# Seven block products in the first layer's second product, and second-layer weights used where they are made

## The chip, the cores and the metric

The kernel runs on one core of a Trainium2 chip. The metric is the device time of one execution in microseconds. A core has five engines with queues of their own, and each works through its queue in program order: TensorE (PE) multiplies matrices, VectorE (DVE), ScalarE (ACT) and GpSimd (POOL) work elementwise, SyncE (SP) issues the transfers between HBM and the on-chip memory SBUF. A matmul writes into one of eight PSUM banks of 128 x 512 fp32, from which ACT and DVE read.

## The reference

```python
def _moe_ref(x, w_in, w_out):                       # first layer, d_ff 2048
    h = x @ w_in
    g = np.maximum(h, 0.0) + np.log1p(np.exp(-np.abs(h)))     # softplus
    return (g @ w_out).astype(np.float32)

def _moe2_ref(x, w_gate, w_val, w_out):             # second layer, d_ff 1536
    g = x @ w_gate
    silu = g * (1.0 / (1.0 + np.exp(-g)))
    val = x @ w_val
    return (silu * val @ w_out).astype(np.float32)

def reference(**kwargs):                            # x (4,8,512,64), state (4,8,32,64)
    attn_out = _attn_ref(**attn_kwargs)             # attention of x and state, both ways
    B, H, S, D = attn_out.shape                     # 4, 8, 544, 64
    x = np.ascontiguousarray(attn_out.transpose(0, 2, 1, 3)).reshape(B * S, H * D)
    x = _moe_ref(x=x, **moe_kwargs)
    return _moe2_ref(x=x, **moe2_kwargs)
```

There are 2176 tokens: 4 batches of 512 positions, and 4 x 32 state rows. The weights come as 64-bit floats.

## The kernel before, in words

Every fp32 operand is split into a high and a low part of a type that PE takes at full rate, and a product is made of three matmuls, high by high, low by high and high by low (`mm3`, L87). All of PE's large products go through its line 90. The high part is a copy on ACT, the low part a subtraction on POOL or DVE (`low`, L92).

After the attention, the first layer runs over 4 chunks c of 512 hidden columns, 4 batches b and 4 tiles ft of a chunk: 64 units of 128 hidden columns by 512 positions. For each unit PE makes `p2` (12 matmuls: the softplus of one unit times a 128-row piece of w_out, into the four banks py, which stay open over the four units of a batch) and `p1` of the unit four steps ahead (6 matmuls into a bank ph). ACT takes the softplus of ph twice, as `h` (high part) and `C` (whole), and POOL subtracts to get `l`. At the end of each batch DVE adds the four banks py to the sums yacc in SBUF (`y_add`, L511). Each chunk also has, for every batch, an M pair (`m_pair`, L442: two groups pm of 8 small matmuls, of the chunk's w_in with the attention's state). Its two banks are one of the tag "m" and one of the tag "h", the tag from which ph takes its banks; ACT copies the high parts and DVE subtracts the low parts (`m_low`, L93) before the banks come free. Products for the state rows (ps) stand at fixed steps too.

Weights are converted in pieces of 128 x 512 by the class `Piece`: ACT scales the upper words (`size`, L135), DVE shifts and joins the words (`head`, L144; `tail`, L155 and L158), ACT and POOL split (L164, L93). 16 pieces each of w_in and w_out belong to the first layer. The second layer's 36 pieces (24 of gate and value, `GatePiece`, 12 of its w_out, `OutPiece`) are made during the first layer (18 of them) or in the first pass of the second (18, by a shorter form: ACT L133, DVE L139 and L151); gate pieces also get four sums of their quarters (L205). A made piece is written to HBM and loaded back when a step needs it (`load_gw`, `load_w2`).

The second layer has 24 steps n: 2 batch pairs by 12 tiles f. Each step makes its gate and value products as seven products of half-size blocks instead of eight (`quad_mm`, P1 to P7), in banks px, py and pz that DVE and ACT empty between them; its output products, too, go by seven parts in the second pass.

The order of work on each engine is the program's: a schedule written by hand. In the first layer `at(n, kind, ...)` hangs work on a unit, and the loop over units emits, for one unit, `p2`, the hooks "pe", `p1`, then for the other engines the softplus of the unit before, `y_add`, and the hooks "dve0", "act", "pool", "dve1" and so on. `M_STEPS` says at which unit of a chunk the M pairs stand. In the second layer `at2` does the same.

```python
    BUFS = {"y": 4, "h": 3, "m": 1}
    LAG = 4
    M_STEPS = (10, 12, 15, 19)
```

## Time and profile before

| | us |
|---|---|
| median of 3 runs | 732.83 (731.96 to 732.92) |
| the profiled execution | 732.92 |
| its span in the profile | 731.1 |
| PE busy | 710.4 (97%) |
| DVE busy | 484.2 (66%) |
| POOL busy | 412.6 (56%) |
| ACT busy | 331.0 (45%) |

The span is what the profiler records between the first and last instruction; 1.8 us of the execution lie around it. The attention takes the first 45 us or so, the first layer goes on to about 320 us, the second layer fills the rest. In the timeline a row that ends with x6 or x12 stands for so many instructions of one kind in sequence. The records of neighbouring instructions of one engine overlap a little, so the distance from start to start is the better measure of what an instruction costs.

### The profile page before, as it was taken

How to read it: one execution, taken by the hardware profiler on the slowest of the kernel's cores; microseconds unless marked ns; L12 is line 12 of the kernel's file. 1: busy time of each engine (PE TensorE's matmuls, PEld its weight loads, DVE VectorE, ACT ScalarE, POOL GpSimd, SP SyncE). 2: the span in 40 equal slices, each digit the busy share in tenths (PEclk: the TensorE clock that was granted, in tenths of full speed). 3: DMA queues.
4: the chain of work that ended last, by engine and by line, in shares of the span. 5: the costliest groups of instructions: out<-in, count | busy, mean ns of one | idle time of the engine just before them, and what ended most of it. 6: DMA issues, size and time to landing. Idle time of an engine off the chain costs nothing.

```text
span 731.1 us, 10299 instructions
## 1 busy us (share of the span) xinstructions
PE 710.4 (97%) x3690; PEld 569.6 (78%) x3690; DVE 484.2 (66%) x689; ACT 331.0 (45%) x612; POOL 412.6 (56%) x349
## 2 busy tenths in 40 slices
...
GB/s 342 408 129 10 48 115 138 201 205 179 162 131 189 188 120 161 161 301 0 122 280 330 373 362 278 327 260 337 207 251 386 345 338 279 296 144 328 168 12 116
DMA packets 55395, 159.54 MB, mean 218 GB/s; under 512 B 6192, under 2 KB 18480, under 8 KB 55344
## 3 DMA queue, kind: packets, MB, share of 16 engines
...
q14 instruction: 22, 0.18, 0.1%
...
## 4 chain that ended last, share of the span: by engine, by line
PE 85%; DVE 8%; POOL 2%; issue 2%; ACT 2%; DMA 1%; SPq 0%; ACTq 0%; DVEq 0%; POOLq 0%
PE py L90 24%; PE px L90 18%; PE po L90 10%; PE ph L90 10%; PE pz L90 9%; PE poP L90 7%; PE pt L90 3%; PE pm L432 2%; PE ps L90 1%; PE ps L565 1%; DMA st<-in_st_dram 1%; DVE t_wo L155 1%; DVE t L351 1%; DVE m L93 1%; DVE m L354 1%
## 5 line engine op out<-in xcount | busy, mean ns | idle before, releaser
L90 PE MATMUL py<-h,wo 128*128 128x512 f32 x512 | 159.1, 391 | 0.6 <-POOL wo L93 0.6
L93 POOL TENSOR_TENSOR l<-C,h 128x512 fp32r<-128x512 f32 x64 | 91.7, 1439 | 78.7 <-ACT C L465 61.9
L90 PEld LDWEIGHTS py<-h,wo 128*128 128x128 f32 x512 | 95.9, 188 | 22.2 <-POOL wo L93 1.4
L90 PE MATMUL ph<-aT,m 128*128 128x512 f32 x384 | 99.9, 396 | 2.7 <-DVE m L93 2.7
L90 PE MATMUL py<-l,wo 128*128 128x512 f32 x256 | 99.9, 390 | 0.0
L90 PEld LDWEIGHTS ph<-aT,m 128*128 128x128 f32 x384 | 70.5, 188 | 28.0 <-issue 5.9
L462 ACT ACTIVATE h<-ph 128x512 fp32r<-128x512 f32 x64 | 38.2, 598 | 108.4 <-PE py L90 101.6
L90 PE MATMUL po<-h,w 128*128 128x512 f32 x224 | 69.7, 392 | 0.0
L90 PE MATMUL px<-T_0s,gw 128*128 128x512 f32 x216 | 60.8, 390 | 0.5 <-ACT cA L1025 0.5
L90 PE MATMUL px<-T_1s,gw 128*128 128x512 f32 x216 | 60.7, 390 | 0.0
L90 PEld LDWEIGHTS py<-l,wo 128*128 128x128 f32 x256 | 48.1, 188 | 10.2
L643 DVE TENSOR_TENSOR oacc<-po,oacc 128x512 f32<-128x512 f32 x48 | 32.4, 687 | 27.9 <-PE po L90 27.8
L90 PEld LDWEIGHTS po<-h,w 128*128 128x128 f32 x224 | 41.6, 188 | 8.4
L93 POOL TENSOR_TENSOR gv<-t_gv,gv 128x512 fp32r<-128x512 f32 x24 | 32.4, 1348 | 27.4 <-ACT gv L164 27.2
L643 DVE TENSOR_TENSOR oacc<-poP,oacc 128x512 f32<-128x512 f32 x62 | 40.7, 686 | 10.3 <-PE poP L90 10.3
L90 PEld LDWEIGHTS px<-T_0s,gw 128*128 128x128 f32 x216 | 40.4, 188 | 9.1 <-ACT cA L1025 1.0
L90 PEld LDWEIGHTS px<-T_1s,gw 128*128 128x128 f32 x216 | 40.6, 188 | 8.4
L90 PE MATMUL po<-l,w 128*128 128x512 f32 x112 | 43.7, 390 | 0.0
L93 POOL TENSOR_TENSOR split_gv<-sums_gv,split_gv 128x512 fp32r<-128x512 f32 x24 | 33.1, 1378 | 17.2 <-ACT split_gv L209 16.5
L93 POOL TENSOR_TENSOR l<-cA,h 128x512 fp32r<-128x512 f32 x14 | 19.7, 1407 | 40.0 <-ACT h L629 39.8
L985 POOL TENSOR_TENSOR cC<-cC,cB 128x512 f32<-128x512 f32 x24 | 31.8, 1326 | 18.4 <-ACT cB L984 18.4
L1051 DVE TENSOR_TENSOR cA<-py,cA 128x512 f32<-128x512 f32 x22 | 15.2, 689 | 40.2 <-PE py L90 34.1
...
## 6 DMA issues: line engine op xcount, KB each, us to landing
...
```

The source lines that it names most:

```text
L90: nc.tensor.matmul(o, a[s], b[t], start=first and i == 0, stop=last and i == 2, **k)
L93: eng.tensor_tensor(out=o, in0=whole, in1=high.bitcast(F32), op=ALU.subtract)
L155: nc.vector.scalar_tensor_tensor(out=ti, in0=self.top, scalar=-0x80000000, in1=ti, op0=ALU.bitwise_and, op1=ALU.bitwise_or,)
L351: nc.vector.transpose(self.t, self.sc)
L354: nc.vector.tensor_reduce(out=self.mine("m1", 16), in_=self.t3, op=ALU.max, axis=AX.X)
L432: nc.tensor.matmul(ps[k * NS:(k + 1) * NS, :], st[q, k, b, :], win[c, k].t[q, :], start=True, stop=True)
L462: nc.scalar.activation(self.h, self.ps, AF.Softplus)
L565: nc.tensor.matmul(gs[c][:, f], win[c, kt].t[:, f], sw[:, kt, :], start=kt == 0, stop=kt == KT - 1)
L643: nc.vector.tensor_tensor(out=v, in0=ps, in1=v, op=ALU.add)
L985: nc.gpsimd.tensor_tensor(out=c["C"], in0=c["C"], in1=c["B"], op=ALU.mult)
L1051: nc.vector.tensor_tensor(out=c["A"], in0=y, in1=c["A"], op=ALU.add)
```

## The change

Three stretches of the first layer, each a chunk c and a pair q of batches, (1, 1), (2, 1) and (3, 0), no longer run `p2`. Of their eight units, seven make one block product each (`y_part`, 12 matmuls into two banks pyP), in the order P1, P2, P5, P3, P6, P7, P4, and the eighth makes none. The blocks are the hidden tiles 0, 1 against 2, 3 and the two batches of the pair. This takes sums of the softplus blocks, T1 to T4 (`g_sum`, on DVE, 24 in all), sums of w_out blocks (`WoSums`, on DVE), and their high and low parts on ACT and POOL. Where a batch's two second-batch units with ft < 2 are only used in sums, their own `h` and `l` are left out. Parts P1, P2 and P5 open banks, the others go on adding in a bank which another part has filled, after DVE has added its content to yacc (`y_part_add`).

Of the second layer's 36 pieces, 7 are made in the first layer instead of 18, and 29 in the second layer's first pass instead of 18; these stay in SBUF and are used from there in that pass, and written to HBM for the second pass. The M pairs move to other units and to two banks of the tag "m"; `p1` runs up to seven units ahead of the rest; weight loads start one unit later.

```diff
-    SLOTS = {"aT": 8, "mt": 8,  "wo": 6, "yacc": 8, "s": 2, "xT": 8, "T": 14, "made": 3, "w2": 4, "w2s": 4, "gw": 8}
+    SLOTS = {"aT": 10, "mt": 8,  "wo": 6, "yacc": 8, "s": 2, "xT": 8, "T": 14, "made": 3, "w2": 5, "w2s": 4, "ws": 6}
...
-    BUFS = {"y": 4, "h": 3, "m": 1}
+    BUFS = {"y": 5, "h": 5, "m": 2}
...
+            return "aT" if self.slope else "made"
+
         def low(self):
             super().low()
+            if self.slope:
+                gw[self.f, self.i, 0] = self.out
...
-                gw[n, i, kind] = slot([P, 2, 512], F32R, "gw", f"gw{n}_{i}_{kind}")
+                gw[n, i, kind] = slot([P, 2, 512], F32R, "aT", f"gw{n}_{i}_{kind}")
...
+        if (c, b // 2) in SEVEN and b % 2 and ft < 2:
+            sp[u] = Softplus(ps, g, None)
+        else:
+            sp[u] = Softplus(ps, g, work.tile([P, 512], F32R, tag="GH", bufs=BIG, name=f"h{n}"))
...
+    def y_put(b, dt, ps, first):
         if (b, dt // 2) not in yacc:
             yacc[b, dt // 2] = slot([P, 2, 512], F32, "yacc", f"yacc{b}_{dt // 2}")
         v = yacc[b, dt // 2][:, dt % 2, :]
-        if c == 0 and dt % 2:
-            nc.scalar.activation(v, yps[dt], AF.Copy)
-        elif c == 0:
-            nc.vector.tensor_copy(v, yps[dt])
+        if first and dt % 2:
+            nc.scalar.activation(v, ps, AF.Copy)
+        elif first:
+            nc.vector.tensor_copy(v, ps)
         else:
-            nc.vector.tensor_tensor(out=v, in0=yps[dt], in1=v, op=ALU.add)
+            nc.vector.tensor_tensor(out=v, in0=ps, in1=v, op=ALU.add)
...
+    SEVEN = {(1, 1), (2, 1), (3, 0)}
+    BIG = 16
+
+
+    OUTS = {
+        "P1": ("f0", 0, "B11"), "P2": ("f1", 0, "B21"), "P3": ("s", 3, "B22"), "P4": ("f1", 1, "T4"),
+        "P5": ("s", 0, "T1"), "P6": ("s", 1, "T2"), "P7": ("s", 2, "T3"),
+    }
+    KEEP = {"P1": "x", "P6": "x", "P7": "x", "P4": "x", "P2": "z", "P5": "z", "P3": "z"}
+    OPENS = ("P1", "P2", "P5")
+    TO = {"P1": (0, 0), "P2": (0, 0), "P5": (1, 1), "P6": (1, 0), "P3": (1, 0), "P7": (1, 1), "P4": (0, 1)}
...
+        x, y, op, at = {
+            "T1": ("B12", "B11", ALU.subtract, None), "T3": ("B22", "B12", ALU.subtract, "B12"),
+            "T2": ("T3", "B11", ALU.add, "B11"), "T4": ("B21", "T2", ALU.subtract, "B21"),
+        }[t]
+        a, b = (g_whole(c, q, k, f) for k in (x, y))
+        if at is None:
+            o = work.tile([P, 512], F32, tag="G", bufs=BIG, name=f"{t}_{c}_{q}_{f}g")
+        else:
+            o = g_whole(c, q, at, f)
+        nc.vector.tensor_tensor(out=o, in0=a, in1=b, op=op)
+        gsum[c, q, t, f] = o
...
+        nc.scalar.activation(h, gsum[c, q, t, f], AF.Copy)
+        gT[c, q, t, f] = (h, l)
+
+    def g_split_low(c, q, t, f, eng):
+        h, l = gT[c, q, t, f]
+        low(eng, l, gsum[c, q, t, f], h)
...
+    def y_part(c, q, part):
+        kind, k, t = OUTS[part]
+        keep = KEEP[part]
+        for i in range(2):
+            if part in OPENS:
+                ypx[keep, i] = bank("y", f"pyP{part}_{c}_{q}_{i}")
+            ps = ypx[keep, i]
+            cols = slice(k % 2 * 256 + i * P, k % 2 * 256 + (i + 1) * P)
+            for f in range(2):
+                if t in BLOCK:
+                    j, ft = BLOCK[t]
+                    g = gT[c, 2 * q + j, ft + f]
+                else:
+                    g = gT[c, q, t, f]
+                w = ws[c, k // 2, f] if kind == "s" else wo[c, 2 * int(kind[1]) + f].out
+                mm3(
+                    ps, [w[:, l, cols] for l in range(2)], g, part in OPENS and f == 0, f == 1,
+                    skip_group_check=True,
+                )
+
+    def y_part_add(c, q, part, i):
+        j, m = TO[part]
+        y_put(2 * q + j, 2 * m + i, ypx[KEEP[part], i], c == 0 and part in ("P1", "P5", "P6", "P4"))
...
+    SEQUENCE = ("P1", "P2", "P5", "P3", "P6", "P7", "P4", None)
     LAG = 4
-    M_STEPS = (10, 12, 15, 19)
-    with tc.manual_schedule(engines={ENG.PE}):
+    LEAD = [min(LAG + max(0, n - 11) // 2, 7) for n in range(64)]
+    M_STEPS = (7, 9, 12, 16)
...
-            at(max(0, n - 4), "load", begin)
+            at(max(0, n - 3), "load", begin)
...
+                if i in (5, 7) and SEVEN & {(c + 1, 0), (c + 1, 1)}:
+                    sums = WoSums(c + 1, i // 2 - 2)
+                    m = n + 2 if (c + 1, 0) in SEVEN else n + 7
+                    at(m, "dve1", sums.sums)
+                    at(m + 1, "act", sums.high)
+                    at(m + 1, "pool", sums.low)
             if c + 1 < NCK:
-                for b, i in enumerate(M_STEPS):
+                for b, i in enumerate(M_STEPS if c else (10, 11, 13, 17)):
...
-        EARLY = [(c * UC + n, 0) for c in range(NCK - 1) for n in ((2, 3, 6, 7, 10, 14) if c else (11, 14, 15))]
-        EARLY += [((NCK - 1) * UC + n, 0 if n % 4 else 2) for n in (0, 1, 2)]
-        for j, (n, late) in enumerate(EARLY):
-            at_weights(n, late, made, (j,), second_piece)
-            at(n + late + 1, "pool", lambda j=j: made[j,].sums())
-            at(n + late + 2, "act", lambda j=j: made[j,].split_sums())
...
+        for c, q in sorted(SEVEN):
+            m = c * UC + q * 2 * FT
+            for t, f, n, kind in (
+                ("T1", 0, -1, "dve2"), ("T1", 1, 0, "dve0"), ("T3", 0, 0, "dve2"), ("T2", 0, 1, "dve0"),
+                ("T3", 1, 1, "dve2"), ("T2", 1, 2, "dve0"), ("T4", 0, 2, "dve2"), ("T4", 1, 3, "dve0"),
+            ):
+                at(m + n, kind, g_sum, c, q, t, f)
+            for t, f, n in (
+                ("T1", 0, -1), ("T1", 1, 0), ("T2", 0, 1), ("T2", 1, 2), ("T3", 0, 2), ("T3", 1, 3),
+                ("T4", 0, 3), ("T4", 1, 4),
+            ):
+                at(m + n, "act1", g_split_high, c, q, t, f)
+                at(m + n, "pool1", g_split_low, c, q, t, f, nc.gpsimd)
+        EARLY = [(c * UC + n, 0) for c, n in ((1, 2), (1, 3), (1, 6), (2, 2), (2, 3), (2, 6), (3, 2))]
+        for key, (n, late) in zip(((0, 0), (0, 1), (1, 0), (1, 1), (2, 0), (2, 1), (0, 2)), EARLY):
+            at_weights(n, late, made, key, second_piece)
+            at(n + late + 1, "pool", lambda key=key: made[key].sums())
+            at(n + late + 2, "act", lambda key=key: made[key].split_sums())
...
+            done = FIRST + LAG - 1
+            fresh = []
             for n in range(FIRST, NU):
                 run(n, "load")
-                if True:
-                    u = units[n]
+                u = units[n]
+                c, q, k = u[0], u[1] // 2, n % (2 * FT)
+                seven = (c, q) in SEVEN
+                part = SEQUENCE[k] if seven else None
+                if part:
+                    y_part(c, q, part)
+                elif not seven:
                     p2(u)
-                    if n == FIRST:
-                        p1(units[n + LAG - 1])
-                    run(n, "pe")
-                    if n + LAG < NU:
-                        p1(units[n + LAG])
-                nx = units[n + LAG - 1] if n + LAG - 1 < NU else None
-                if nx:
-                    sp[nx].high()
-                    sp[nx].whole()
-                last = u[2] == FT - 1
-                for dt in range(KT) if last else ():
+                ready, fresh = fresh, []
+                if n == FIRST:
+                    p1(units[done])
+                    ready, done = [units[done]], done + 1
+                run(n, "pe")
+                while done < min(NU, n + LEAD[n] + 1):
+                    p1(units[done])
+                    fresh.append(units[done])
+                    done += 1
+                for v in ready:
+                    sp[v].high()
+                    sp[v].whole()
+                for dt in range(KT) if not seven and u[2] == FT - 1 else ():
                     y_add(u[0], u[1], dt)
                 run(n, "dve0")
+                if part:
+                    y_part_add(c, q, part, 0)
                 run(n, "act")
-                if nx:
-                    g_low(nx)
+                for v in ready:
+                    g_low(v)
                 run(n, "pool")
+                run(n, "dve2")
+                if part:
+                    y_part_add(c, q, part, 1)
...
+        for f in range(NF):
+            for part, t0 in enumerate((4 * f - 8, 4 * f - 7, 4 * f - 5 if f > 1 else 2)):
+                if (f, part) in made:
+                    continue
+
+                def begin(f=f, part=part):
+                    made[f, part] = second_piece(f, part, True)
+
+                at2(t0 // 4 - 1, "load", begin)
...
-        for q, n in enumerate((10, 12, 13, 14, 16)):
+        for q, n in enumerate((11, 12, 14, 16, 18)):
...
-                if n + 2 < NS2:
+                if n == 0 or NF <= n + 2 < NS2:
                     load_gw(n + 2)
-                if n % 2 and n + 1 < NS2:
+                if n % 2 and NF <= n + 1 < NS2:
...
```

PE, third unit of batch 2 of chunk 1 before the change (py1_2_3 is a bank of chunk 1, batch 2; pm2 the M pair of chunk 2; ph the first product):

```order
L90 MATMUL py1_2_3_1754<-l1_2_2_1741,wo1_2_1379 128x512
L432 MATMUL pm2_0_0_1843<-t_win2_0_1399,st_81 32x512
L432 MATMUL pm2_0_0_1843<-t_win2_1_1443,st_81 32x512
L432 MATMUL pm2_0_0_1843<-t_win2_2_1573,st_81 32x512
L432 MATMUL pm2_0_0_1843<-t_win2_3_1635,st_81 32x512
L432 MATMUL pm2_0_1_1848<-t_win2_0_1399,st_81 32x512
L432 MATMUL pm2_0_1_1848<-t_win2_1_1443,st_81 32x512
L432 MATMUL pm2_0_1_1848<-t_win2_2_1573,st_81 32x512
L432 MATMUL pm2_0_1_1848<-t_win2_3_1635,st_81 32x512
L90 MATMUL ph1_3_2_1853<-aT3_0_932,m1_3_0_1556 128x512 x3
L90 MATMUL ph1_3_2_1853<-aT3_1_934,m1_3_1_1558 128x512 x3
L90 MATMUL py1_2_0_1751<-h1_2_3_1731,wo1_3_1321 128x512 x2
```

PE after the change, from the last unit of batch 1 of that chunk on, where the same M pair (pm2_0) now stands:

```order
L90 MATMUL py1_1_3_1569<-l1_1_3_1505,wo1_3_1362 128x512
L446 MATMUL pm2_0_0_1712<-t_win2_0_1367,st_81 32x512
L446 MATMUL pm2_0_0_1712<-t_win2_1_1408,st_81 32x512
L446 MATMUL pm2_0_0_1712<-t_win2_2_1564,st_81 32x512
L446 MATMUL pm2_0_0_1712<-t_win2_3_1628,st_81 32x512
L446 MATMUL pm2_0_1_1717<-t_win2_0_1367,st_81 32x512
L446 MATMUL pm2_0_1_1717<-t_win2_1_1408,st_81 32x512
L446 MATMUL pm2_0_1_1717<-t_win2_2_1564,st_81 32x512
L446 MATMUL pm2_0_1_1717<-t_win2_3_1628,st_81 32x512
L90 MATMUL ph1_3_2_1722<-aT3_0_926,m1_3_0_1455 128x512 x3
L90 MATMUL ph1_3_2_1722<-aT3_1_928,m1_3_1_1457 128x512 x3
L90 MATMUL pyPP1_1_1_0_1757<-h1_2_0_1451,wo1_0_1205 128x512 x2
```

The M pair moved three units forward, out of batch 2 and to the end of batch 1, ahead of the first part of the stretch.

DVE in the same stretch before the change, from the end of batch 2 on (yacc2 are the sums of batch 2, m2 the M pair's low parts):

```order
L511 TENSOR_TENSOR yacc2_0_1156<-py1_2_0_1751,yacc2_0_1156 128x512
L511 TENSOR_TENSOR yacc2_0_1156<-py1_2_1_1752,yacc2_0_1156 128x512
L511 TENSOR_TENSOR yacc2_1_1159<-py1_2_2_1753,yacc2_1_1159 128x512
L511 TENSOR_TENSOR yacc2_1_1159<-py1_2_3_1754,yacc2_1_1159 128x512
L93 TENSOR_TENSOR m2_0_0_1867<-pm2_0_0_1843,m2_0_0_1867 128x512
L93 TENSOR_TENSOR m2_0_1_1869<-pm2_0_1_1848,m2_0_1_1869 128x512
L144 TENSOR_SCALAR t_wo2_2_1941<-t_wo2_2_1941 128x512
```

DVE after the change, from the sums of the softplus blocks for T2 and T3 to the second bank of P5 (C are softplus blocks, overwritten by sums; pyPP1 is the bank of part P1, and so on):

```order
L598 TENSOR_TENSOR C1_2_0_1450<-C1_3_0_1651,C1_2_0_1450 128x512
L533 TENSOR_TENSOR yacc2_0_1150<-pyPP2_1_1_0_1804,yacc2_0_1150 128x512
L598 TENSOR_TENSOR C1_3_1_1693<-C1_3_3_1778,C1_3_1_1693 128x512
L533 TENSOR_TENSOR yacc2_0_1150<-pyPP2_1_1_1_1811,yacc2_0_1150 128x512
L155 SCALAR_TENSOR_TENSOR t_wo2_2_1796<-raw_wo2_2_1672,t_wo2_2_1796 128x512
L158 SCALAR_TENSOR_TENSOR t_wo2_2_1796<-raw_wo2_2_1672,t_wo2_2_1796 128x512
L93 TENSOR_TENSOR m2_1_0_1842<-pm2_1_0_1818,m2_1_0_1842 128x512
L93 TENSOR_TENSOR m2_1_1_1844<-pm2_1_1_1823,m2_1_1_1844 128x512
L598 TENSOR_TENSOR C1_2_1_1492<-C1_3_1_1693,C1_2_1_1492 128x512
L533 TENSOR_TENSOR yacc3_1_1357<-pyPP5_1_1_0_1858,yacc3_1_1357 128x512
L598 TENSOR_TENSOR C1_2_2_1542<-C1_2_2_1542,C1_2_0_1450 128x512
L533 TENSOR_TENSOR yacc3_1_1357<-pyPP5_1_1_1_1865,yacc3_1_1357 128x512
```

Where four additions and two low parts stood, additions from banks now alternate with sums of blocks, and a weight piece's tail and an M pair stand between P2's and P5's.

PE after the change, the second bank of P5 and the first of P3 (hT1 and lT1 are the split T1; P3 uses the tile that P5 opened, so its rows bear the name pyPP5):

```order
L90 MATMUL pyPP5_1_1_1_1865<-hT1_1_1_0_1753,ws1_0_0_1501 128x512 x2
L90 MATMUL pyPP5_1_1_1_1865<-lT1_1_1_0_1754,ws1_0_0_1501 128x512
L90 MATMUL pyPP5_1_1_1_1865<-hT1_1_1_1_1798,ws1_0_1_1656 128x512 x2
L90 MATMUL pyPP5_1_1_1_1865<-lT1_1_1_1_1799,ws1_0_1_1656 128x512
L90 MATMUL ph2_0_1_1872<-aT0_0_473,m2_0_0_1736 128x512 x3
L90 MATMUL ph2_0_1_1872<-aT0_1_428,m2_0_1_1738 128x512 x3
L90 MATMUL pyPP5_1_1_0_1858<-h1_3_2_1730,ws1_1_0_1503 128x512 x2
L90 MATMUL pyPP5_1_1_0_1858<-l1_3_2_1792,ws1_1_0_1503 128x512
L90 MATMUL pyPP5_1_1_0_1858<-h1_3_3_1779,ws1_1_1_1658 128x512 x2
L90 MATMUL pyPP5_1_1_0_1858<-l1_3_3_1846,ws1_1_1_1658 128x512
```

Between P5's last matmul and P3's first stand the six of one ph; P3's first comes behind DVE's addition from the same bank, the row `yacc3_1_1357<-pyPP5_1_1_0_1858` above.

## Rows read from the trace of the kernel before

**Rows 1.** Page, part 1: engine, busy us, share of the span, count.

```profile
PE 710.4 (97%) x3690; PEld 569.6 (78%) x3690; DVE 484.2 (66%) x689; ACT 331.0 (45%) x612; POOL 412.6 (56%) x349
```

**Rows 2.** Chain that ended last: start us, us, engine, what, count.

```profile
199.69 2.72 PE py L90 x12
```

**Rows 3.** Waits of PE: engine, line, waited for, us, times, longest.

```profile
PE ph L90 <- DVE m L93: 2.7, 3, 1.3
```

**Rows 4.** Timeline of PE, two stretches: start us, us, instruction, [idle before <-releaser].

```profile
184.55 1.63 PE L90 MATMUL ph<-aT,m 128*128 128x512 f32 x6 [0.70 <-DVE m L93]
...
262.38 1.62 PE L90 MATMUL ph<-aT,m 128*128 128x512 f32 x6 [0.76 <-DVE m L93]
```

**Rows 5.** Timeline of DVE before the first of those waits.

```profile
181.33 2.48 DVE L511 TENSOR_TENSOR yacc<-py,yacc 128x512 f32<-128x512 f32 x4
...
183.72 1.28 DVE L93 TENSOR_TENSOR m<-pm,m 128x512 fp32r<-128x512 f32 x2
```

**Rows 6.** Timeline of PE: a batch end, and around an M pair.

```profile
162.29 1.52 PE L90 MATMUL ph<-aT,m 128*128 128x512 f32 x6
...
174.55 0.39 PE L90 MATMUL py<-l,wo 128*128 128x512 f32 x1
...
175.89 1.65 PE L90 MATMUL ph<-aT,m 128*128 128x512 f32 x6
```

**Rows 7.** Timeline of DVE around the end of batch 1 of chunk 1.

```profile
157.37 1.00 DVE L144 TENSOR_SCALAR t_w<-t_w 128x512 int32<-128x512 int32 x1 [2.48 <-ACT t_w L135]
...
160.10 1.66 DVE L158 SCALAR_TENSOR_TENSOR t_win<-raw_win,t_win 128x512 int32<-128x512 int32 x1
...
163.01 2.48 DVE L511 TENSOR_TENSOR yacc<-py,yacc 128x512 f32<-128x512 f32 x4
...
165.40 0.92 DVE L144 TENSOR_SCALAR t_gv<-t_gv 128x512 int32<-128x512 int32 x1
```

**Rows 8.** Timeline of DVE, twelve microseconds later.

```profile
175.52 1.77 DVE L155 SCALAR_TENSOR_TENSOR t_wo<-raw_wo,t_wo 128x512 int32<-128x512 int32 x1
...
180.72 0.69 DVE L158 SCALAR_TENSOR_TENSOR t_gv<-raw_gv,t_gv 128x512 int32<-128x512 int32 x1
```

**Rows 9.** Timeline of POOL in the same stretch.

```profile
175.28 3.17 POOL L93 TENSOR_TENSOR l<-C,h 128x512 fp32r<-128x512 f32 x2
...
181.31 1.27 POOL L93 TENSOR_TENSOR l<-C,h 128x512 fp32r<-128x512 f32 x1 [1.18 <-ACT C L465]
```

**Rows 10.** Groups of DVE by line and shape: busy us, mean ns, idle before.

```profile
L155 DVE SCALAR_TENSOR_TENSOR t_wo<-raw_wo,t_wo 128x512 int32<-128x512 int32 x14 | 17.9, 1276 | 0.1
...
L158 DVE SCALAR_TENSOR_TENSOR t_wo<-raw_wo,t_wo 128x512 int32<-128x512 int32 x14 | 14.0, 1000 | 0.5
...
L205 DVE TENSOR_TENSOR sums_gv<-t_gv 128x128 f32<-128x128 f32 x24 | 10.5, 436 | 0.0
...
L144 DVE TENSOR_SCALAR t_wo<-t_wo 128x512 int32<-128x512 int32 x14 | 10.8, 779 | 19.9 <-ACT t_wo L135 19.8
...
L151 DVE SCALAR_TENSOR_TENSOR t_gv<-t_gv,raw_gv 128x512 int32<-128x512 int32 x12 | 10.1, 843 | 0.4 <-ACT t_gv L133 0.3
...
L531 DVE TENSOR_TENSOR T<-T,yacc 128x512 f32<-128x512 f32 x4 | 4.6, 1140 | 0.0
...
L527 DVE TENSOR_TENSOR T<-yacc,yacc 128x512 f32<-128x512 f32 x4 | 3.9, 974 | 0.0
```

**Rows 11.** Windows, line 980 alone: stretch, us, DVE busy (count), clock, DMA share.

```profile
59.00:731.00 672.00, 16.43 (x20) 1.00 0.61 213
```

**Rows 12.** Windows: stretch, us, PE, PEld, DVE, ACT, POOL busy, clock, DMA.

```profile
144.40:178.40 34.00, 34.00 (x160) 26.72 (x159) 27.03 (x32) 16.78 (x31) 27.14 (x27) 1.00 0.58 205
...
375.00:392.00 17.00, 17.00 (x83) 14.34 (x82) 10.94 (x21) 7.16 (x13) 10.58 (x8) 1.00 0.81 281
```

**Rows 13.** Timeline of a second-layer step: an ACT copy and PE after it.

```profile
373.11 0.58 ACT L1025 ACTIVATE cA<-px 128x512 f32<-128x512 f32 x1
...
373.74 0.97 PE L90 MATMUL px<-T_0s,gw 128*128 128x512 f32 x3 [0.53 <-ACT cA L1025]
```

137 lines of the change are left out of this document (87 added, 50 removed).

## The prediction

> **What bounds the kernel now.** I read the page's busy shares first: PE is busy for 710.4 of 731.1 us, DVE for 66%, POOL for 56%, ACT for 45% [rows 1]. What counts is therefore how many matmuls PE issues and where it stands still. The mean of a matmul record there, 0.39 us, is no price, since records overlap; the chain of waits gives it: twelve matmuls of py take 2.72 us from start to start, 0.2267 us each [rows 2]. The clock of that part of the trace is 1.00, the 2.4 GHz level [rows 12]. Next I read what PE waits for. Behind the attention there is one entry of size, ph waiting for DVE's subtraction m, 2.7 us in three waits [rows 3]. So before the change nearly everything off PE is hidden. The question is whether it still is when PE has less to do and DVE more.
>
> **What the change removes.** A stretch of eight units takes 8 x 12 = 96 matmuls of py; now seven parts take 7 x 12 = 84. Three stretches save 36 matmuls, 36 x 0.2267 = 8.16 us, all of it on PE, hence on the path.
>
> Two of the three waits for m also go. At 184.55 and 262.38 us ph waits 0.70 and 0.76 us [rows 4]: it needs a bank that the M pair filled, and DVE releases it with two subtractions at 183.72 us, queued behind four additions of yacc that began at 181.33 [rows 5]. In the new order the pair stands three units earlier, and its subtractions come several microseconds ahead of the next use: gain 1.46 us. The third wait is in chunk 0, which keeps its layout; I let it stand. The price of the early place is that PE comes to the pair at 162.29 us [rows 6], while the last weight it needs is joined on DVE by 160.10 + 1.66 = 161.76 [rows 7]; margin 0.5 us. The order on DVE ahead of that is the same, so I cost it at nothing; if the cover went, up to 0.5 us would be lost there and regained at the wait below, since PE would then reach P3 later.
>
> **What it adds on DVE, and the new wait.** Per stretch DVE gets eight sums of two SBUF blocks (128 x 512), eight small sums of weights, and 14 additions from banks instead of eight. Two stretches saw most of their second-layer pieces taken off DVE in exchange. What matters is the row "yacc3_1<-pyPP5_1_1_0" of the order: P3 adds into the bank that P5 has just filled, so PE cannot start P3 before DVE has added P5 to yacc. Between P5's first bank and P3 PE has only 12 matmuls, 2.7 us. All other turns of the sequence (P6 to P7, P7 to P4) have as much and fewer DVE instructions before them. So I add up both engines from the end of batch 1 of chunk 1 to P3.
>
> PE: from 162.29 us on, two M pairs and 60 matmuls (ph, P1, ph, P2, ph, P5, ph: 6 + 12 + 6 + 12 + 6 + 12 + 6). An M pair costs 175.89 - 174.55 - 0.23 = 1.11 us [rows 6]. 162.29 + 2.22 + 13.60 = 178.1 us.
>
> DVE: its four additions for the batch begin at 163.01 us [rows 7]; with the small weight sums partly in the 2.48 us in which DVE idled before 157.37 [rows 7], I start at 163.4. Then, in the new order, it has
> - four additions, 2.39 us (165.40 - 163.01 by rows 7, 0.60 each);
> - five more single additions from banks and four subtractions m, at the same 0.60: 5.4 us;
> - six block sums. Their nearest rows are other sums with two operands in SBUF, of the same shape: 16.43 us for 20 on line 980 [rows 11], 4.6 for four and 3.9 for four on lines 531 and 527 [rows 10], in all 24.9 / 28 = 0.889 us. 5.33 us;
> - two heads at 0.779, 1.56 us, and one tail, 1.276 + 1.000 = 2.28 us [rows 10].
>
> Sum 16.96, end 180.4 us: PE waits 2.3 us. Chunk 2's stretch has the same order, 2.3 us more. In chunk 3 PE has 66 matmuls and one M pair from the last part of chunk 2's stretch to P3, 16.1 us; DVE has in that time, by the order, nine operations at 0.60, six sums (5.33), one tail (2.28), one head (0.78) and four sums of half the size at half the price (1.78), 15.6 us; wait 0. New waits 4.6 us.
>
> The bounds come from how long the two-operand work takes. A tail instruction took 0.69 us at 180.72 and 1.77 at 175.52 [rows 8]. POOL was at work on `l` over the second, and idle for 1.18 us up to 181.31 over the first [rows 9]. Low end: six sums at 0.69, the tail at 2 x 0.69, two heads at 0.7: 2.39 + 5.4 + 4.1 + 1.4 + 1.4 = 14.7, end 178.1, no wait. High end: sums at 1.14 [line 531, rows 10], heads at 1.00 [rows 7], the tail at 2 x 1.77: 2.39 + 5.4 + 6.84 + 2.0 + 3.54 = 20.2, end 183.6, wait 5.5 us. I take the mean, because POOL is busy 27.14 of 34.0 us in that stretch [rows 12] and neither always nor never beside a sum.
>
> Here a rule speaks against the change. The Trainium skill, "SBUF — State Buffer", section "Who interferes with whom", says that DVE and GpSimd share a port pair under an exclusive lock, that a DVE instruction with two SBUF inputs contends for it with a GpSimd instruction that reads SBUF, and that the loser waits until the other is done; with one SBUF input it doesn't contend. The trace agrees: 0.69 against 1.77 us, while additions with a bank as one operand keep 0.60. By the rule the added sums are of just the kind that is held up.
>
> **The other added work** has cover. ACT gets 24 high parts of T and 12 of weight sums less six, POOL as many low parts; both give up the second-layer pieces of the first layer. In the stretch ACT is busy 16.78 of 34.0 us [rows 12]. One `l` more on POOL per unit fits only because gate pieces go; if that failed, a late lT would hold P5, P6 or P7, whose margins are one unit, some 4 us.
>
> **The second layer's first pass** makes 29 pieces instead of 18. Per gate piece DVE adds about 0.78 + 0.84 + 4 x 0.436 = 3.4 us, per piece of w_out 1.6 us [rows 10]: six and five more, 28 us over some ten steps, 3 us a step. In 375 to 392 us DVE is busy 10.94 of 17.0 us, POOL 10.58, ACT 7.16 [rows 12]; 13.9 of 17 still fits. But PE waits once there already: px at 373.74 us stood 0.53 us for ACT's copy of px, which began at 373.11 behind conversions [rows 13]. If one such wait came per step, 10 x 0.53 = 5.3 us. Below: the wait goes, -0.5. I take one more of them, +0.5 us, since eleven further pieces fall on steps with room. Fewer loads back are worth nothing, because PE nowhere waits for one there. The later weight loads and the changed steps of the output sums have no wait beside them either.
>
> **Sum** against the profiled execution, 732.92 us (span 731.1 and 1.8 around it; the median of the runs is 732.83, 0.1 away): 732.92 - 8.16 - 1.46 + 4.6 + 0.5 = **728.4 us**.
>
> **The rivals.**
> - DVE keeps up: sums at 0.69 where POOL is idle. No wait at P3: 732.92 - 9.62 = 723.3, with up to 1 us of odd waits 724. For it: a wait elsewhere delays PE and gives DVE time. Against it: POOL busy for 0.8 of the stretch.
> - Slower: DVE's two-operand instructions are nearly all held up by POOL. Then PE waits 5.5 us at P3 in chunks 1 and 2, and about 3 in chunk 3 (sums 6 x 0.25, the tail 1.26, head and small sums 0.7, less the margin of 0.5): 14. 732.92 - 9.62 + 14 + 0.5 = 737.8 us. It decides from where the three waits pass 9.1 us: some 0.2 us more than my mean on each of the ten two-operand or head instructions of a run-up. The rule of the Trainium skill named above stands for this case; the means of before, which hold both kinds, against it.
> - A wash by the second layer: each of ten steps of the first pass has the wait of 373.74 us. 728.4 - 0.5 + 5.3 = 733.2 us. For it: that wait is there with 18 pieces. Against it: one alone in the pass.
> - That the change doesn't do what it says can be left out: the order has 36 rows of matmuls less.
>
> **How the numbers follow.** About 0.2%, 1.5 us, is what a measurement of this kernel can tell from no change: 731.4 to 734.3. My forecast of 728.4, with its own range 726.5 to 731, has 0.42; full gain near 723.5, 0.18; the wash, 0.13; the slower case, 0.27, to which mixed mishaps of the same mechanism in the second layer belong. Faster 0.42 + 0.18 = 0.60, same 0.13, slower 0.27. The range of 8 in 10 reaches from the full gain to the slower case: 723.3 to 738.
>
> **What would show it.** Right: PE waits on DVE yacc just ahead of P3, once each near 178 and 256 us, 1 to 4 us long, none ahead of P6, P7 and P4; the waits of ph for m down to one; matmuls of py and pyP at 0.227 us apart; the L598 sums at 0.7 to 1.2 us in the mean; at most one or two waits in the first pass of the second layer. Wrong: waits of PE for POOL's lT or for ACT's softplus in the stretches (a unit of lead is then too little), block sums above 1.2 us, or waits of px, py or pz at every step between 320 and 480 us.

## The result and the profile after

The changed kernel takes 743.32 us (median of four runs, 742.58 to 743.80) against 732.88 before: 1.0141 times as long, 95% interval 1.0124 to 1.0159. The forecast was 728.4 us, range 723.3 to 738. It is slower by 10.4 us where 4.4 us of gain were forecast.

The page of the profile after, part 1 (engine, busy us, share of the span), and of part 2 (forty slices of the span) PE, DVE and the granted clock:

```profile
PE 710.4 (96%) x3654; PEld 567.1 (76%) x3654; DVE 548.0 (74%) x768; ACT 345.5 (47%) x641; POOL 456.1 (61%) x355
...
PE   5699999999899979899999999999999999999997
...
DVE  5875553789679897958489988889785666665564
...
PEclk9899999999899999999999999999999999999999
```

Against [rows 1]: PE has 36 matmuls fewer and is as long busy, which already says that some of them ran slowly, and PE has dents in the 11th, 15th and 17th slice, where DVE is full or was full in the slice ahead. Over the whole kernel DVE has 64 us more work, POOL 43.5. The list of PE's waits (line, waited for, us in all, times, longest) names the place:

```profile
PE pyPP L90 <- DVE yacc L533: 10.7, 3, 4.2
...
PE pm L446 <- DVE m L93: 1.2, 1, 1.2
...
PE ph L90 <- DVE m L93: 0.2, 1, 0.2
```

Of the three waits of [rows 3] the two of [rows 4] are gone, as forecast. The third, in the start of the kernel, is 0.2 us instead of 1.3, but there pm now waits 1.2 us for m instead of 0.3. The new one is the one that was forecast, ahead of P3 in each of the three stretches, but with 10.7 us instead of 4.6. PE's timeline around the first of them, in chunk 1 (start, us, instruction, idle before):

```profile
182.70 1.53 PE L90 MATMUL ph<-aT,m 128*128 128x512 f32 x6
188.42 1.22 PE L90 MATMUL pyPP<-h,ws 128*128 128x512 f32 x2 [4.19 <-DVE yacc L533]
189.44 0.63 PE L90 MATMUL pyPP<-l,ws 128*128 128x512 f32 x1
189.87 1.05 PE L90 MATMUL pyPP<-h,ws 128*128 128x512 f32 x2
...
193.71 4.04 PE L687 MATMUL ps<-sw,t_win 128*128 128x128 f32 x32
```

P3's twelve matmuls take 193.71 - 188.42 = 5.29 us instead of the 2.72 of [rows 2]. The windows show why (stretch, us, busy times, granted clock in the third column from the right):

```profile
180.00:184.00 4.00, 4.00 (x18) 2.91 (x16) 3.97 (x5) 1.39 (x3) 4.00 (x3) 1.00 0.40 131
188.40:194.00 5.60, 5.58 (x14) 4.42 (x15) 5.57 (x6) 2.15 (x5) 5.49 (x4) 0.50 0.09 26
...
197.00:200.00 3.00, 3.00 (x18) 2.56 (x17) 0.47 (x2) 2.22 (x5) 0.00 (x0) 1.00 0.00 0
...
270.00:274.00 4.00, 4.00 (x12) 3.21 (x13) 3.97 (x5) 1.54 (x4) 4.00 (x3) 0.65 0.00 0
...
310.00:315.00 5.00, 4.71 (x14) 3.72 (x15) 4.97 (x6) 0.64 (x2) 4.16 (x3) 0.66 0.00 0
```

Ahead of the wait the clock is 1.00, behind it 0.50, the 1.2 GHz level, later 1.00 again. Chunks 2 and 3 show the same after waits of 4.21 and 2.27 us (0.65 in 270 to 274 us, 0.66 in 310 to 315). So each wait is paid a second time. An estimate from these three windows of what the clock takes: 5.60 x 0.50 + 4.00 x 0.35 + 5.00 x 0.34 = 5.9 us.

Why DVE is late is read by laying two timelines beside each other, DVE (first) and POOL, in the run-up to P3 in chunk 1:

```profile
174.24 0.68 DVE L598 TENSOR_TENSOR T_1g<-C,C 128x512 f32<-128x512 f32 x1
174.84 0.68 DVE L533 TENSOR_TENSOR yacc<-pyPP,yacc 128x512 f32<-128x512 f32 x1
175.44 1.19 DVE L598 TENSOR_TENSOR C<-C,C 128x512 f32<-128x512 f32 x1
...
177.98 1.77 DVE L598 TENSOR_TENSOR C<-C,C 128x512 f32<-128x512 f32 x1
...
183.21 1.66 DVE L158 SCALAR_TENSOR_TENSOR t_wo<-raw_wo,t_wo 128x512 int32<-128x512 int32 x1
...
185.99 1.78 DVE L598 TENSOR_TENSOR C<-C,C 128x512 f32<-128x512 f32 x1
187.69 0.68 DVE L533 TENSOR_TENSOR yacc<-pyPP,yacc 128x512 f32<-128x512 f32 x1
```

```profile
174.25 1.83 POOL L93 TENSOR_TENSOR lT<-T_0g,hT 128x512 fp32r<-128x512 f32 x1
176.04 1.73 POOL L93 TENSOR_TENSOR split_gv<-sums_gv,split_gv 128x512 fp32r<-128x512 f32 x1
177.74 1.46 POOL L93 TENSOR_TENSOR l<-C,h 128x512 fp32r<-128x512 f32 x1
179.17 1.75 POOL L93 TENSOR_TENSOR lT<-T_1g,hT 128x512 fp32r<-128x512 f32 x1
...
182.58 1.74 POOL L93 TENSOR_TENSOR lT<-C,hT 128x512 fp32r<-128x512 f32 x1
184.28 1.72 POOL L93 TENSOR_TENSOR l<-C,h 128x512 fp32r<-128x512 f32 x1
185.96 1.25 POOL L93 TENSOR_TENSOR wo<-t_wo,wo 128x512 fp32r<-128x512 f32 x1
```

A DVE instruction with two operands in SBUF that begins while one of POOL's is running ends 0.6 us after a boundary of POOL's: 175.44 + 1.19 = 176.63 by 176.04; 179.75 by 179.17; 184.87 by 184.28; 187.77 by 185.96 + 1.25 = 187.21. It takes as long as POOL's running instruction still has to go, and 0.6 of its own. The sum at 174.24 us, which began just before POOL's lT, took 0.68. All 66 additions from banks to yacc take 0.67 to 0.69 us, whatever POOL does. POOL pays too: 1.7 us where [rows 9] had 1.27 beside additions from banks on DVE ([rows 5]).

The heads (L144), with one operand in SBUF, are held up as well. Between the stretches one took 0.43 us at 279.62, with POOL idle; beside POOL's `l` one ended 0.28 us after POOL's boundary at 309.36:

```profile
308.15 1.49 DVE L144 TENSOR_SCALAR t_w<-t_w 128x512 int32<-128x512 int32 x1
```

```profile
307.64 1.72 POOL L93 TENSOR_TENSOR l<-C,h 128x512 fp32r<-128x512 f32 x1
```

One part of the difference varies from run to run. The first py starts at 46.38 us in this trace and at 45.40 in the one of before; over the changed kernel and its variants below, whose orders of work are the same up to there, at 44.1 to 47.4. Where it matters I therefore compare the stretch from the first py to the first px of the second layer: 301.6 us before, 309.7 after. (The first layer ends, by this measure, at 347.0 us before, not at about 320.)

### The profile page after: what moved, and what is told of

The parts are those of the page before. It is cut to its first block, busy times and chain, and to the rows that moved or that the text cites. A ratio compares the mean times of both kernels' runs of the same rounds, so it can differ in the third digit from the quotient of the medians.

```text
span 742.0 us, 10249 instructions
## 1 busy us (share of the span) xinstructions
PE 710.4 (96%) x3654; PEld 567.1 (76%) x3654; DVE 548.0 (74%) x768; ACT 345.5 (47%) x641; POOL 456.1 (61%) x355
## 4 chain that ended last, share of the span: by engine, by line
PE 76%; DVE 15%; ACT 3%; issue 2%; POOL 2%; DMA 1%; SPq 0%; DVEq 0%; ACTq 0%
PE px L90 16%; PE py L90 16%; PE po L90 8%; PE ph L90 8%; PE pz L90 8%; PE poP L90 6%; PE pyPP L90 5%; PE pt L90 3%; DVE C L598 2%; PE ps L687 2%; DVE yacc L533 2%; PE pm L446 1%; PE ps L90 1%; DVE m L93 1%; DVE t_wo L155 1%
## 5 line engine op out<-in xcount | busy, mean ns | idle before, releaser
L93 POOL TENSOR_TENSOR l<-C,h 128x512 fp32r<-128x512 f32 x58 | 83.8, 1449 | 48.1 <-ACT C L480 42.7
L90 PE MATMUL py<-h,wo 128*128 128x512 f32 x320 | 99.4, 391 | 0.9 <-POOL wo L93 0.8
L90 PEld LDWEIGHTS py<-h,wo 128*128 128x128 f32 x320 | 60.0, 188 | 14.5 <-POOL wo L93 1.6
L90 PE MATMUL py<-l,wo 128*128 128x512 f32 x160 | 62.3, 390 | 0.0
L477 ACT ACTIVATE h<-ph 128x512 fp32r<-128x512 f32 x58 | 34.4, 592 | 42.4 <-PE ph L90 42.3
L480 ACT ACTIVATE C<-ph 128x512 f32<-128x512 f32 x64 | 38.0, 594 | 9.0 <-PE ph L90 9.0
L90 PE MATMUL px<-T_0s,gw 128*128 128x512 f32 x135 | 38.1, 390 | 0.7 <-ACT cA L1177 0.7
L90 PE MATMUL px<-T_1s,gw 128*128 128x512 f32 x135 | 38.0, 389 | 0.0
L533 DVE TENSOR_TENSOR yacc<-pyPP,yacc 128x512 f32<-128x512 f32 x42 | 28.4, 683 | 8.9 <-PE pyPP L90 8.9
L90 PEld LDWEIGHTS py<-l,wo 128*128 128x128 f32 x160 | 30.0, 188 | 6.3
```

The source lines that it names most:

```text
L90: nc.tensor.matmul(o, a[s], b[t], start=first and i == 0, stop=last and i == 2, **k)
L93: eng.tensor_tensor(out=o, in0=whole, in1=high.bitcast(F32), op=ALU.subtract)
L477: nc.scalar.activation(self.h, self.ps, AF.Softplus)
L480: nc.scalar.activation(self.g, self.ps, AF.Softplus)
L533: nc.vector.tensor_tensor(out=v, in0=ps, in1=v, op=ALU.add)
```

## The experiments

Every kernel is the changed one with the edit shown or told. "To before" is the ratio to runs of the kernel before that were made beside it; their medians lie between 732.88 and 733.76 us. "First layer" is that stretch of its trace, one execution of each kernel: for after it is the slowest of four, for p5_first the fastest of ten.

| kernel | median us | to before | 95% interval | first layer us |
|---|---|---|---|---|
| before | 732.88 | 1 | | 301.6 |
| after | 743.32 | 1.0141 | 1.0124 to 1.0159 | 309.7 |
| p5_first | 732.35 | 0.9985 | 0.9971 to 0.9999 | 298.0 |
| filled | 736.74 | 1.0053 | 1.0035 to 1.0071 | 302.8 |
| no_seven | 729.47 | 0.9941 | 0.9924 to 0.9958 | 299.1 |
| no_low_T | 735.13 | 1.0022 | 1.0009 to 1.0035 | 301.3 |
| no_low_all | 725.68 | 0.9895 | 0.9880 to 0.9909 | 291.0 |
| gates_moved | 736.87 | 1.0054 | 1.0037 to 1.0071 | 302.3 |
| gates_moved_p5_first | 733.19 | 0.9993 | 0.9981 to 1.0004 | 298.5 |
| low_on_dve | 738.18 | 1.0059 | 1.0044 to 1.0074 | 304.2 |
| pieces_chunk0 | 739.20 | 1.0085 | 1.0071 to 1.0099 | 308.1 |
| two_stretches | 740.17 | 1.0097 | 1.0083 to 1.0111 | 305.7 |
| pieces_spread | 739.71 | 1.0080 | 1.0064 to 1.0096 | 305.2 |
| stretches_1_and_3 | 729.14 | 0.9937 | 0.9919 to 0.9954 | 295.3 |
| m_three | 729.77 | 0.9952 | 0.9935 to 0.9970 | 296.4 |
| h_six | 729.63 | 0.9943 | 0.9922 to 0.9964 | 296.5 |

**p5_first**: the place of the wait.

```diff
+                first = part == "P5"
+                for i in range(2) if first else ():
+                    y_part_add(c, q, part, i)
                 run(n, "dve0")
-                if part:
+                if part and not first:
                     y_part_add(c, q, part, 0)
...
-                if part:
+                if part and not first:
                     y_part_add(c, q, part, 1)
```

> DVE adds P5's two banks to yacc ahead of the M pair's low parts and of the block sum for T2, not behind them. Theory A (P3 waits for DVE's addition of P5, which stands in a queue that is some 4 us late; while PE stands still its clock falls, which costs about 2 us more each time): in chunks 1 and 2 the addition comes about 2.9 us earlier (two subtractions of 0.6 and one sum of 1.7 us), so the waits ahead of P3 shrink from 4.2 to about 1.3 us, in chunk 3 from 2.3 to under 1.5, the clock stays at 1.00 behind them, and the time falls by some 6 to 7 us for the waits and 5 to 6 for the clock, to 731 to 733 us. Rival B (the loss is outside the three stretches, in the changed start, M pairs or second layer): no more than 2 us are won, 741 us or more. Rival C (DVE is behind as a whole, so the wait only moves): P6 now waits for T2 by as much, and the time stays above 739 us.

732.35 us. No wait ahead of P3 is longer than 1.3 us (chunk 3 has none there; its 0.7 us stands at P5's second bank), and the clock is 1.00 in 183.3 to 187 us and in 274.5 to 279, behind the longest wait. Of rival C a part came true: ahead of P7 in chunk 2 PE waits 2.1 us for P6's addition. Moving two additions per stretch on one engine's list gives back 11 us, and all of the loss.

```profile
PE pyPP L90 <- DVE yacc L533: 5.4, 4, 2.1
```

**filled**: the clock.

```diff
-                    p1(units[done])
+                    p1(units[done], (2 if c == 3 else 4) if part == "P5" else 1)
```

> The product ph that stands ahead of P3 is computed four times over in chunks 1 and 2 and twice in chunk 3: 42 matmuls more, 9.5 us of work for PE at 0.227 us, put where it stood still. Theory A (the clock falls to its lower level because PE stands still for 4 us): P3 starts at the same times as before, as DVE sets them, but at clock 1.00, its twelve matmuls take 2.7 us instead of 5.3, and the kernel gets faster by 4 to 6.5 us in spite of more work: 737 to 739 us. Rival D (the clock in these stretches falls for another reason, such as how busy all engines are): P3 still runs at 0.43 us a matmul, 743 us or more. Rival E (the waits aren't idle time of PE that can be filled): about 9.5 us slower, 752 us.

736.74 us, 6.6 less than the changed kernel with 42 matmuls more. In chunk 1 P3 starts right behind the four products ph, at 187.93 us, and its twelve matmuls take 190.65 - 187.93 = 2.72 us (PE first, then DVE):

```profile
182.49 5.60 PE L90 MATMUL ph<-aT,m 128*128 128x512 f32 x24
187.93 0.61 PE L90 MATMUL pyPP<-h,ws 128*128 128x512 f32 x2
...
190.65 1.61 PE L687 MATMUL ps<-sw,t_win 128*128 128x128 f32 x13
...
185.79 0.67 DVE L598 TENSOR_TENSOR C<-C,C 128x512 f32<-128x512 f32 x1
186.38 0.68 DVE L533 TENSOR_TENSOR yacc<-pyPP,yacc 128x512 f32<-128x512 f32 x1
```

So DVE did not set the start of P3 there, though theory A said it would: this time DVE's sum took 0.67 us instead of 1.78, and P5's first bank was added at 187.06, 0.9 us before PE was ready. In chunk 3 a wait of 0.9 us was left. Matmuls added (9.5 us) and wait left come to 10.5 us, where the waits were 10.7, so nearly all of the gain is the clock: about 6.6 us, near the 5.9 estimated from the windows. Theory A holds against D and E: the clock falls because PE stands still.

**no_seven**: the rest of the change alone.

```diff
-            self.t = rawp.tile([P, 512], F32, tag=f"t{self.tag}", bufs={"win": 8, "wo": 5}.get(self.tag, 3), name=f"t_{self.name}")
+            self.t = rawp.tile([P, 512], F32, tag=f"t{self.tag}", bufs={"win": 7, "wo": 5}.get(self.tag, 3), name=f"t_{self.name}")
...
-    SEVEN = {(1, 1), (2, 1), (3, 0)}
+    SEVEN = set()
```

> The set of stretches is empty (all batches go by py as before the change), with the rest of the change kept: 29 of the second layer's pieces made in its first pass, the M pairs and loads at their new places (one buffer less for weights in the making, for room). Theory A: 8.2 us of matmuls come back, the waits ahead of P3 (11.1 us) and the slow clock behind them (about 6.5) go: 733 to 735 us, and what is left over the kernel before is the start of the first layer (1.6 us) and the second layer (about 0.6). Rival B (the second layer's 29 pieces, or the new places, cost most of it): 740 us or more.

729.47 us, better than either theory said and faster than before. The first layer is 2.5 us shorter than before, 1.5 of it the waits of [rows 4]; where the other 1.0 comes from is open. The second layer, from its first px to the last matmul, takes 380.6 us where it took 380.0, so its changes, eleven more pieces among them, cost about 0.6 us. By the medians the seven products thus cost 14 us, and the rest of the change wins 3.4. Of the 14 the two traces show 10.6 in the first layer; 2.0 lie in the start and 1.2 behind the last matmul, and whether the products cause these is open.

**no_low_T** and **no_low_all**: what makes DVE late. The first:

```diff
-        l = work.tile([P, 512], F32R, tag="GL", bufs=BIG, name=f"l{t}_{c}_{q}_{f}")
         nc.scalar.activation(h, gsum[c, q, t, f], AF.Copy)
-        gT[c, q, t, f] = (h, l)
+        gT[c, q, t, f] = (h, h)
...
-                at(m + n, "pool1", g_split_low, c, q, t, f, nc.gpsimd)
```

> Leaves out the low parts of the block sums T1 to T4: POOL doesn't compute them, and PE multiplies by the high part in their place (as many matmuls). DVE's list of work is unchanged; POOL has eight operations of 1.3 to 1.8 us less per stretch. Theory A1 (DVE's two-operand work is late because POOL's instructions hold it up): the sums on line 598 fall from a mean of 1.27 us to below 1.0, the waits ahead of P3 to under half (below 5 us in all three together), and the time to 728 to 735 us. Rival F (DVE has too many instructions, whatever POOL does): the sums stay at 1.2 us or more, the waits at 9 us or more in all, 741 us or more.

735.13 us; two waits of 3.3 us were left, the third was gone, and the sums took 1.085 us: between A1 and F.

```profile
PE pyPP L90 <- DVE yacc L533: 6.7, 2, 3.3
```

So the second takes the softplus blocks' low parts as well:

```diff
+        if (u[0], u[1] // 2) in SEVEN:
+            gT[u] = (sp[u].h, sp[u].h)
+            return
```

> Leaves out every low part that POOL makes of the softplus blocks and of their sums in the three stretches; PE multiplies by the high part in their place, as many matmuls. DVE's list is as in the changed kernel, and POOL keeps only the weights' low parts and sums there. (Without the low parts of T alone the waits ahead of P3 had fallen from 10.7 to 6.7 us, between the two expectations.) Theory A1 (a DVE instruction with two operands in SBUF ends 0.6 us after the POOL instruction beside which it began, so POOL's work sets DVE's pace): block sums at 0.8 us or less in the mean, waits ahead of P3 under 2 us in all, no fall of the clock, 723 to 729 us. Rival F (DVE has too many instructions): sums at 1.1 us or more, waits of 5 us or more, 733 us or more.

725.68 us and no wait for yacc. The sums over blocks, in the changed kernel and here (mean ns in the second number behind the bar):

```profile
L598 DVE TENSOR_TENSOR C<-C,C 128x512 f32<-128x512 f32 x18 | 22.8, 1269 | 0.0
```

```profile
L601 DVE TENSOR_TENSOR C<-C,C 128x512 f32<-128x512 f32 x18 | 14.9, 827 | 0.0
```

The sums are a little above A1's 0.8 us and far below F's 1.1. DVE's list is the same, so F as it was put (whatever POOL does) falls: POOL's work is what makes DVE late. The first layer is 291.0 us here and 299.1 without stretches: 8.1 us, the 36 matmuls at 0.2267 us. That is what the seven products take off the first layer where PE doesn't wait for DVE's additions. Of the whole time it is 3.8 us by the medians (725.68 against 729.47): in these two traces the start is 2.9 us later (47.33 against 44.38) and the second layer 0.5 longer. And the low parts that are left out here belong to the result, so this kernel shows a cause and is no way out.

**low_on_dve**: p5_first, with T's low parts on DVE.

```diff
-                at(m + n, "pool1", g_split_low, c, q, t, f, nc.gpsimd)
+                at(m + n + 1, "dve0", g_split_low, c, q, t, f, nc.vector)
```

> P5's additions first, and the eight low parts of T per stretch made on DVE instead of POOL. DVE gets eight instructions more, POOL eight fewer. Theory A1 (what two-operand work costs is the time in which POOL holds DVE up): block sums fall to 1.0 us or less in the mean (from 1.18 with P5's additions first), and DVE's eight additional subtractions take 0.6 to 1.0 us each, about what the sums give back: within 2 us of 732.4. Rival F (the number of DVE's instructions decides): 24 x 0.7 = 17 us more work on DVE in stretches where it has no idle time, 738 us or more.

738.18 us.

```profile
L598 DVE TENSOR_TENSOR C<-C,C 128x512 f32<-128x512 f32 x18 | 19.6, 1087 | 0.0
L93 DVE TENSOR_TENSOR lT<-C,hT 128x512 fp32r<-128x512 f32 x18 | 19.2, 1090 | 0.0
```

The block sums got shorter (1.087 us) but not to 1.0, and the low parts themselves took 1.09: A1's sum was wrong, and the number of DVE's instructions counts too. With POOL's `l` still there, both are held up.

**gates_moved**, **gates_moved_p5_first**: the early pieces out of the run-ups; the second has p5_first's edit too.

```diff
-        EARLY = [(c * UC + n, 0) for c, n in ((1, 2), (1, 3), (1, 6), (2, 2), (2, 3), (2, 6), (3, 2))]
+        EARLY = [(c * UC + n, 0) for c, n in ((0, 11), (0, 13), (0, 15), (1, 13), (1, 15), (2, 13), (3, 10))]
```

> Makes the seven early second-layer pieces elsewhere in the first layer: units 11, 13, 15 of chunk 0, 13 and 15 of chunk 1, 13 of chunk 2, 10 of chunk 3, in place of units 2, 3, 6 of chunks 1 and 2 and unit 2 of chunk 3, which lie ahead of the stretches and in them. Nothing else is changed, as many instructions in all. Theory A1: POOL loses six operations and DVE three between the last batch before the stretch and P3; the waits ahead of P3 fall from 4.2 to 1 to 2.5 us in chunks 1 and 2, in chunk 3 from 2.3 to about 1; the clock stays or falls for a shorter time; 729 to 735 us. Rival G (the pieces cost DVE and POOL the same wherever they stand, and the waits move with them): waits elsewhere in the first layer, 739 us or more.

> Both edits, the early pieces elsewhere and P5's additions first. Theory A1: no wait ahead of P3 over 0.7 us, what waits of PE remain in the stretches are under 2 us in all; 724 to 728 us, faster than the kernel before and than the changed kernel without its stretches (729.5 us). Rival C (DVE is behind as a whole and P6 waits for T2): as with P5's additions first alone, 731 us or more.

736.87 and 733.19 us. The waits ahead of P3 fell to 0.9 us at most in the first kernel and were gone in the second, as A1 said, but new ones came in chunk 3: in the first 2.3 us for POOL's wo, 1.3 for lT, and 1.2 us for yacc behind the stretch. About the time A1 was wrong both times; the first lies between A1 and G (735 and 739), and C was right about the second. Two more layouts, both with p5_first's edit, tried to place the pieces better. **pieces_chunk0**: units 11 to 15 of chunk 0, 13 and 15 of chunk 1; **two_stretches** is the same without chunk 3's stretch; **pieces_spread**: units 11, 13, 15 of chunk 0, 13 and 15 of chunk 1, 2 of chunk 2, 7 of chunk 3.

> P5's additions first, and the seven early second-layer pieces at units 11 to 15 of chunk 0 and 13 and 15 of chunk 1, none in chunks 2 and 3. With the pieces at units 13 of chunk 2 and 10 of chunk 3 PE had waited 2.4 us for POOL's wo and 0.9 for lT in chunk 3's stretch and 1.2 us for yacc behind it. Theory A1 (waits come where POOL's and DVE's two-operand work meet ahead of a stretch): those three go, the first layer from 62 us on takes 269 to 271 us (276.4 before the change, 285.4 after it, 274.4 with the former places), and the whole 727 to 730 us, faster than the kernel before by 0.4 to 0.9%. Rival C (DVE is behind as a whole, waits move on): no better than 733 us, and DVE's waits stand in the stretches of chunks 1 or 2.

> As the one with the pieces in chunks 0 and 1 and P5's additions first, but only the stretches (1,1) and (2,1) go by seven parts. 12 matmuls come back, 2.7 us. Theory A1: chunk 3's stretch, with its weight sums next to POOL's, costs less than it saves once the pieces are gone from it, so this is 1 to 3 us slower than with three: 729 to 732 us. Rival H (chunk 3's stretch loses more than 2.7 us in waits): this one is the faster of the two.

> P5's additions first, and the seven early pieces at units 11, 13, 15 of chunk 0, 13 and 15 of chunk 1, 2 of chunk 2 and 7 of chunk 3. Five in a row at the end of chunk 0 had made ph wait 5 us for the softplus there; three at a distance of two units had not. Against the kernel that had pieces at unit 13 of chunk 2 and 10 of chunk 3 its waits for POOL's wo (2.4), for lT (0.9) and for yacc behind chunk 3's stretch (1.2) should go. Theory A1: the first layer from 62 us on takes 269 to 272 us, and the whole 727 to 730 us. Rival C (waits move on wherever the pieces go): 732 us or more.

739.20, 740.17 and 739.71 us: theory A1 missed all three times, by 8 to 10 us. With one stretch less two_stretches is 1.0 us slower than pieces_chunk0; the two are not to be told apart, and rival H, by which it is the faster one, has nothing for it. The waits of pieces_chunk0 and of pieces_spread:

```profile
PE ph L90 <- ACT C L480: 6.4, 2, 5.0
```

```profile
PE py L90 <- DVE yacc L533: 6.3, 2, 4.2
```

In the first, ACT stood 4.0 us for POOL's sums of a piece with the softplus behind it in its queue. In the second, four tail instructions (1.63 to 1.77 us each, beside POOL) stood ahead of the additions that free py's banks in chunk 2. In each of the four layouts tried the pieces make PE wait somewhere; rival C holds in the times, though in pieces_chunk0 not in the place (its longest wait is in chunk 0, for ACT).

**stretches_1_and_3**: p5_first without the stretch of chunk 2, which still had long waits.

```diff
-    SEVEN = {(1, 1), (2, 1), (3, 0)}
+    SEVEN = {(1, 1), (3, 0)}
```

> P5's additions first, the early pieces at their places of the changed kernel, and only the stretches of chunks 1 and 3 by seven parts. With P5's additions first, chunk 1's stretch kept a wait of 1.3 us ahead of P3 and chunk 3's one of 0.7, each less than the 2.7 us that a stretch saves, while chunk 2's had 1.3 and 2.1, more than it saves. Theory A1: the sum by these numbers, from the kernel without stretches (729.5 us): 729.5 - 5.4 + 2.0 = 726 us, 725 to 728. Rival C (a stretch's DVE and POOL work costs as much in places that these waits don't show): 729.5 us or more, so that the seven products are worth nothing here at all.

729.14 us, against 729.47 without stretches: not to be told apart. Its first layer, at 295.3 us, is 3.8 us shorter, as the sum said (3.4); but its first py starts at 47.13 us where the other's starts at 44.38. Is that start a cost of the stretches? **m_three** and **h_six** are stretches_1_and_3 with other PSUM banks; m_three's edit is shown, h_six has "h": 6 and "m": 2 instead:

```diff
-    BUFS = {"y": 5, "h": 5, "m": 2}
+    BUFS = {"y": 5, "h": 5, "m": 3}
```

> The kernel with the stretches of chunks 1 and 3 and P5's additions first, with three instead of two PSUM banks asked for under the tag of the M pairs. In its start, before the first py, the M pair's products wait 1.2 us for DVE's low part of an earlier pair (0.3 before the change), and the clock at 36 to 40 us is at its lower level. Theory S (the changed division of the banks costs about 1 us of wait there, and up to 1 us of clock behind it): that wait falls below 0.5 us, the first py starts at 44.5 to 45.5 us instead of 47.1, and the time falls by 1 to 2 us, to 727 to 728. Rival R (the start differs from run to run whatever the banks): the same 729 us within 0.7, and the first py anywhere between 44 and 47.5 us.

> The same kernel with six instead of five PSUM banks asked for under the tag of ph, which half of an M pair also takes. Theory S: if the wait at the start is for a bank of this tag, it falls below 0.5 us and the time to 727 to 728 us; if it is for one of the other tag, nothing changes here. Rival R: 729 us within 0.7 in either case.

729.77 and 729.63 us. The wait of pm at the start, 1.2 us, is in both; yet the first py starts at 46.47 and 44.38, with a clock at 36 to 40 us of 0.64 and 1.00. As rival R says, the start differs with the same wait; neither edit took the wait away or won time. That kernels with stretches start late more often than the one without can't be excluded from one trace of each; how much of the 1.0 us by which the changed kernel's first py was late is due to the change stays open.

## Why the prediction was wrong

- The matmuls: 8.16 us forecast, 8.1 measured between no_low_all and no_seven. Right.
- The waits for m: 1.46 us, gone as forecast; [rows 4] have no counterpart after.
- The second layer: 0.5 us forecast, 0.6 measured. Right in size, by luck in part: the forecast had a second wait like that of [rows 13]; PE waits there once, 0.7 us instead of 0.5, so 0.4 of the 0.6 stands in no wait of the list.
- "New waits 4.6 us" is the term that was mis-sized: 10.7 us. In chunk 1, PE's side was 0.5 us too short: from the end of the last py (167.51 + 0.23 = 167.74) to a P3 without wait (182.70 + 6 x 0.2267 = 184.06) it is 16.3 us, against 15.8. On DVE's side the additions of the batch began 1.7 us behind that last py (169.44 against 167.74) and not 1.1, as three of the four tail instructions ahead of them took 1.7 us beside POOL; and from there to the end of P5's addition (187.69 + 0.68) it took 18.9 us, not 17.0. These 1.9 us are the two-operand work: from start to start the six block sums took 6.8 us instead of 5.33 and the tail 2.8 instead of 2.28. Chunk 3's "wait 0" failed on the small weight sums: costed at 0.44 us each, three of four took 1.4 to 1.5 beside POOL's wo, lT and `l`:

```profile
294.70 1.40 DVE L566 TENSOR_TENSOR wsum<-wsum,t_wo 128x256 f32<-128x256 f32 x1
296.03 1.51 DVE L566 TENSOR_TENSOR wsum<-t_wo 128x256 f32<-128x256 f32 x1
297.46 1.50 DVE L566 TENSOR_TENSOR wsum<-t_wo,wsum 128x256 f32<-128x256 f32 x1
...
294.48 1.35 POOL L93 TENSOR_TENSOR wo<-t_wo,wo 128x512 fp32r<-128x512 f32 x1 [2.02 <-ACT wo L167]
295.78 1.47 POOL L93 TENSOR_TENSOR lT<-T_0g,hT 128x512 fp32r<-128x512 f32 x1
297.21 1.47 POOL L93 TENSOR_TENSOR l<-C,h 128x512 fp32r<-128x512 f32 x1
```

  The mean of 0.889 us came from 28 sums of which 18 took 0.68 to 0.69 us, as one beside an idle POOL does; the new ones stand where POOL is busiest, with POOL work of their own making, and the 18 sums on C took 1.269 us, above the 1.2 that the prediction named as a sign of being wrong. The rows that told it, [rows 8] and [rows 9], were read, and the waits of 4.2 us in chunks 1 and 2 lie nearer to their high end, 5.5 us, than to the 2.3 of the mean; the mean was the wrong choice.
- A term was missing: what PE loses behind a wait. All prices were for clock 1.00, and no rival had one for its fall. By filled it is 6.6 of the 14.9 us by which the forecast missed, and the waits are 6.1 of them. The slower rival, 14 us of waits at 737.8, had the right mechanism for the waits, with waits a third too long; with the measured ones and this term its sum would be 732.9 - 9.6 + 10.7 + 6.6 + 0.5 = 741.1.
- Sum for the first layer: -8.2 - 1.5 + 10.7 + 6.6 = +7.6 us; measured 309.7 - 301.6 = 8.1. The second layer adds 0.6; the start (1.0) and the end behind the last matmul (5.4 us against 4.2) are the rest of the 10.9 us between the spans.

The rule weighed in the prediction, from the Trainium skill, "SBUF — State Buffer", section "Who interferes with whom" (the loser of the shared port pair waits out the other's whole instruction), is what the two timelines show, boundary by boundary. The prediction's "with one SBUF input it doesn't contend" leaves out the page's condition, "outside the 2-port perf modes", and does not hold for all of this kernel: additions with a bank as operand kept 0.67 to 0.69 us, but heads, with one operand in SBUF, took 0.41 to 1.52. Which mode the heads run in no run here shows. The Trainium skill, "TensorE: Matmul & The Clock Gate", section "HAM oscillation — how this bites in real kernels", warns that pauses of PE take its clock down; the trace agrees with 0.50 behind a wait of 4.19 us; the clock fell behind one of 2.27 us as well (0.66), while in p5_first it stayed at 1.00 behind one of 2.12.
